# Sixteen f chunks of batches 0 and 1 as pairs of seven block products over token halves

## The chip, the cores and the metric

The kernel runs on one core of one Trainium2 chip. The metric is the device time of one execution in microseconds, lower is better. The engines are named as in the profile: PE (matrix products), DVE (vector), ACT (activations), POOL, SP (here a DMA queue).

## What is computed

Sigmoid attention over 8 batches, 12 heads, 448 tokens, head size 64, followed by a gated feed-forward layer on 3584 tokens (d_model 768, d_ff 1536):

```python
scores = scale * q @ k.T - log(S);  attn = 1 / (1 + exp(-scores))
x = (attn @ v) with the heads side by side          # 3584 x 768
out = (maximum(x @ w_gate, 0) * (x @ w_val)) @ w_out
```

## The kernel before

Everything is in fp16 with fp32 sums in PSUM, which is eight banks of 512 fp32 columns; `bank(name)` takes the next bank of a ring, and `later` moves banks to the ring's end. The schedule is written by hand: on each engine, instructions run in the order in which the code issues them, and tiles carry the waits between engines.

**Attention.** A unit is one key chunk of 64 tokens of a group of four heads: `qk_unit` writes the scores of 448 queries into two banks (L238), and two sigmoids on ACT (L186) bring them to SBUF as PT. A batch has 21 units, three groups of seven. `pv` (L256) multiplies a group's seven PT with v, and `put_xT` on DVE (L183) writes the transposed result xT: 6 chunks of 128 model columns by 448 tokens.

**Rounds.** Batch b's units are cut into six bursts (for b = 1 of 3, 3, 3, 4, 4, 4 units; later of 4, 3, 4, 3, 4, 3), some with a pv of the group before in them. After each burst, PE does feed-forward work of earlier batches, until the next burst; `jobs` are other steps (loads, rel copies and DMA transposes of the next batch, sums) that go along with that work. The queue `gv_queue` holds the direct feed-forward chunks, `ffn_mix(n)` does n of them, `next_work` does the next entry of `work`, and `prepare` makes the sums for the entry after.

**Direct chunks.** For one of the 12 f chunks (128 columns of d_ff), `gv_product` (L321) makes the gate and the value, each six matmuls into a bank of its own; ACT takes the Relu (L333) and DVE multiplies (L342) into hT. Batch 0's tokens are taken in parts of 256 and 192, batch 1's in one of 448.

**Seven products.** Batches 2 to 7 are taken two at a time: gate and value weights, and the two halves of d_model, make a 2 x 2 block matrix, and two batches the other side. `gv_pair` does two f chunks with seven block products (Strassen's scheme in Winograd's form, L408) in place of eight. Its sums of weights come from `gate_sums` (in place in wv) and `unit_sums` on DVE (L399, L571), those of tokens from `batch_sums`. Three PSUM banks per chunk, u (called b in the code), g2 (c) and g1 (a), are copied or added into SBUF tiles gsb (L616, L620) between products; the first copy is on DVE (on ACT at the end of the kernel), the next two on ACT.

**Down.** `down_pair` does the same for the last product, two tiles of 128 tokens at a time, with four sums of w_out (`weight_sums`, tile T) and `token_sums` on DVE. Work entries are ("w", g, f) for `gv_pair`, ("y", g, p) for `down_pair`, and ("t", g, 6) for tile 6, which is left over and goes through `down` (L369) directly. g counts pairs of batches.

**Around the change.** Batches 0 and 1 are all direct: 20 queue entries of batch 0 in b = 1's rounds (4, 3, 3, 3, 3, 4), nine chunks of batch 1 in b = 2's (2, 2, 1, 1, 1, 2), three in b = 3's (1, 1, 1, then tile 6, then y1). `down_pair` y0 follows the last two chunks of b = 2. The token sums for y0 are made in b = 2's third round, weight sum 0 in its fifth, 1 and 2 in its sixth, 3 beside y0. `dma_transposes` are two copies to a tile rel on DVE (L221) and a DMA transpose on SP. `hold` makes POOL wait for such a transpose before it issues the next loads.

Of the kernel before, what the change touches and what calls it, by code (L numbers as in the profile page):

```python
# [10 lines left out]
FP32 = mybir.dt.float32  # L11
# [6 lines left out]
def kernel(  # L18
# [332 lines left out]
    def store(g, t, ysb, m0, m1, engines):  # L351
        if (g, t) in ((0, 0), (0, 1)):
            put_off.append((g, t, ysb, m0, m1, engines))
        else:
            stored(g, t, ysb, m0, m1, engines)
# [8 lines left out]
    def down(g, t):  # L364
        ysb = ysbp.tile([P, DM], FP32, tag="ysb", name="ysb")
        for nm, m0, m1 in (("ya", 0, 512), ("yb", 512, DM)):
# [12 lines left out]
        store(g, t, ysb, 0, DM, (nc.sync, nc.sync))  # L379

    HF, HM, HD = NFC // 2, DM // 2, NDC // 2
    late = {}
# [170 lines left out]


    def gate_sums(f0, f1):
        fs = slice(f0 * P, f1 * P)
        sub(wv[:, 0:HD, fs], wg[:, 0:HD, fs], wv[:, 0:HD, fs])

    def unit_sums(g, f):
        S1, S2, S4 = sums_tile(2 * P)
# [6 lines left out]
        sums[("w", g, f)] = S1, S2, S4  # L573

    def batch_blocks(g, ks):
        x1, x2 = xT_tiles[2 * g], xT_tiles[2 * g + 1]
# [13 lines left out]
    def gv_pair(g, f, beside, first_copy):  # L590
# [67 lines left out]
        else:  # L658
# [2 lines left out]
            gated_first()  # L661
            gated_second(0, 2 * NPP * P - S)

    gv_queue = deque()

    def push_gv(b, q0, qn, fs, act_relu=True):
# [4 lines left out]
        c0, c1 = HALVES[half]  # L671
        push_gv(0, 64 * c0, 64 * (c1 - c0), fs, act_relu)

    def ffn_mix(count, hooks=()):
        hooks = list(hooks)
        for left in range(count, -1, -1):
            while hooks and hooks[0][0] >= left:
                hooks.pop(0)[1]()
            if left:
                gv_queue.popleft()()  # L680


    nc.scalar.activation(gate[:], zeros[:, 0:2], AF.Sigmoid, bias=sig_bias, scale=qk_scale)
# [63 lines left out]
                after[(i, u)]()  # L747
    slots[5].pv()
    push_first(1, range(0, 4))
    for f0 in range(4, 12, 2):  # L750
        for half in range(2):
            push_first(half, range(f0, f0 + 2))


    order = [(g, c) for g in range(NG) for c in range(NCH)]

    def pv_finish(b):
        pv_group(b, NG - 1)
        if b < 2:
            push_gv(b, 0, S, range(NFC))  # L760

    first_psum.close()
    open_banks("ring1")
# [4 lines left out]
    def both(b, g):  # L768
        pe_transposes(b, g, 0)
        pe_transposes(b, g, 1)  # L770
# [5 lines left out]
        load_o()  # L776


    work = deque()

    pending = []

    def push_group(g):
        tail = [("y", g, p) for p in range(3)]
        if g != 2:
            tail.insert(0, ("y", g, NPP) if g == 3 else ("t", g, 2 * NPP))
        if g == 0:
            tail.insert(0, tail.pop(1))
        work.extend([("w", g, f) for f in range(0, NFC, 2) if g > 0] + tail)

    def prepare():
        if work:
            kind, g, i = work[0]
            if kind == "w":
                unit_sums(g, i)
            elif kind == "y":
                token_sums(g, i, 0, HF - 2 if FRESH.get(g) == i else HF)

    def next_work(jobs=(), alone=False, first_act=False, amid=None):
        kind, g, i = work.popleft()  # L800

        due = pending[:]
        del pending[:]

        def beside():
            for job in due + list(jobs):
                job()

        if kind == "y":
            down_pair(g, i, beside, prepare, not work, scaled_act if alone or first_act else scaled, amid)  # L810
        elif amid:
            raise ValueError(kind)
        elif kind == "w":
            gv_pair(g, i, lambda: (prepare(), beside()), nc.scalar.copy if alone else nc.vector.tensor_copy)
        else:
            beside()
            prepare()
            down(g, i)

    for b in range(1, B):  # L820
        if b == 1:
            cuts, pv_at = (0, 3, 6, 9, 13, 17, 21), {3: (0, 2), 5: (1, 2)}
        else:
            cuts, pv_at = (0, 4, 7, 11, 14, 18, 21), {0: (-1, 2), 2: (0, 2), 4: (1, 2)}
        bursts = list(range(len(cuts) - 1))
        inner = {}
        if b > 2:
            inner = {0: 1} if b % 2 == 0 else {2: 3, 3: 5} if b == B - 1 else {4: 5}
            for n in inner.values():
                bursts.remove(n)  # L830
        count = len(bursts)
        hooks = {}
        if b == 1:
            mix = (4, 3, 3, 3, 3, 4)
            hooks = {
                1: [(3, lambda: both(1, 1))],
                3: [(3, lambda: both(1, 2))],
                4: [(3, lambda: dma_transposes(2, 0)), (1, lambda: dma_transposes(2, 1))],
                5: [(4, late_loads)],
            }  # L840
        elif b == 2:
            mix = (2, 2, 1, 1, 1, 2)
            hooks = {
                2: [(0, prepare)],
                4: [(0, lambda: weight_sums(0))],
                5: [(1, lambda: weight_sums(1)), (0, lambda: weight_sums(2))],
            }
            open_late()
        elif b == 3:
            mix = (1, 1, 1, 0, 0)  # L850
        else:
            mix = (0,) * count

        def burst(n):
            for i, (g, c) in enumerate(order[cuts[n] : cuts[n + 1]]):
                if n in pv_at and i == pv_at[n][1]:
                    if n == 0:
                        pv_finish(b - 1)
                        if b == 2:
                            push_group(0)  # L860
                        elif b % 2 == 0:
                            push_group(b // 2 - 1)
                    else:
                        pv_group(b, pv_at[n][0])
                qk_unit(b, g, c)

        if b == 3:
            dma_transposes(3, 2)
            for args in put_off:
                stored(*args)  # L870
        for m in range(count):
            jobs = []
            burst(bursts[m])
            if m == 0 and b > 3:
                jobs.append(lambda: dma_transposes(b, 2))
            if b == 2 and m == count - 1:
                jobs.append(lambda: (dma_transposes(3, 0), dma_transposes(3, 1)))
            elif b == 3 and m == count - 1:
                jobs.append(lambda: dma_transposes(4, 1))
            elif 0 <= m - count + 2 and 3 < b < B - 1:  # L880
                jobs.append(lambda: dma_transposes(b + 1, m - count + 2))
            if b == 1:
                if m == 0:
                    load(2, 0, 1, "kq")
                    load(2, 1, 2, "kq")
                    load(2, 2, 3, "kq")
            elif m == 0 and b + 1 < B:
                if b == 3:
                    jobs.append(lambda: hold(3, 2))
# [8 lines left out]
            if b == 2 and m == count - 1:  # L898
                ffn_mix(mix[m], hooks[m])
                next_work(jobs + [lambda: weight_sums(3)], first_act=True)  # L900
            elif mix[m]:
                for job in jobs:
                    job()
                ffn_mix(mix[m], hooks.get(m, ()))
            else:
                next_work(jobs, amid=(lambda: burst(inner[m])) if m in inner else None)
            if b == 3 and m == count - 2:
                dma_transposes(4, 0)
            if b == 3 and m in (1, 3):
                for f in range(*((0, 8, 2), (8, NFC, 2))[m // 2]):  # L910
                    gate_sums(f, f + 2)
    pv_finish(B - 1)
    push_group(B // 2 - 1)
    next_work([lambda: batch_sums(B // 2 - 1, (1, HD))])
# [32 lines left out]
```

## Time and profile before

| | |
|---|---|
| median of 3 runs | 391.92 us (391.62 to 392.65) |
| span of the profiled execution, first to last instruction | 390.9 us |
| the profiled execution's own time beside it | not shown; the runs lie 0.7 to 1.7 us above the span |
| PE, DVE, ACT, POOL busy | 384.7, 283.4, 228.4, 50.1 us |
| granted PE clock | 0.998 |

The parts of the span by stage, with PE's busy time from the windows view: first batch's attention 0 to 29.7 us (27.5), b = 1's rounds 29.7 to 62.3 (32.6, no idle), b = 2's 62.3 to 98.9 (36.6, no idle), b = 3's 98.9 to 135.7 with y1 in it (36.8, no idle), later rounds to 303.5 (167.8 of 167.8), and the end without attention (83.4 of 87.4). In profile lines an engine's idle time and what ended it stand in brackets, "x6" is the number of instructions in a row, and L321 is line 321 of the kernel.

### The profile page before, as it was taken

To read this page: it belongs to the slowest core of one execution; us is meant where nothing else is said; L and a number is where in the kernel's file an instruction comes from. 1 tells how busy PE (TensorE), PEld (TensorE's weight loads), DVE (VectorE), ACT (ScalarE), POOL (GpSimd) and SP (SyncE) were. 2 spreads that over 40 slices of the span, in tenths; PEclk is the share of its full clock that TensorE was granted. 3 is DMA by queue.
4 is the path that set the end of the run, shared out by engine and by line. 5 is a ranking of instruction groups with operands and counts; after the bars stand their busy time and mean duration, and the time that the engine had idled before them with its cause. 6 is when DMAs were issued, how large, how long until landed. Compare 5 with 4: busy or idle time off the path is not lost.

```text
span 390.9 us, 8798 instructions
## 1 busy us (share of the span) xinstructions
PE 384.7 (98%) x3504; PEld 218.0 (56%) x3504; DVE 283.4 (73%) x560; ACT 228.4 (58%) x483; POOL 50.1 (13%) x74
## 2 busy tenths in 40 slices
PE   8999999999999999999999999999999999999995
PEld 6678776445455545454555554545455555555663
DVE  3453444358387789999757789999987788999563
ACT  5967786784877755555556774545467354333321
POOL 8643404300320300003000300000000000000000
PEclk9999999999999999999999999999999999999999
DMA  9999997996998992225946696132003220000335
GB/s 174 198 199 204 204 186 120 205 204 111 194 185 166 140 236 37 49 47 58 195 93 115 136 198 108 24 67 41 14 18 74 74 80 2 0 3 0 81 88 155
DMA packets 68985, 43.79 MB, mean 112 GB/s; under 512 B 35664, under 2 KB 65616, under 8 KB 68944
## 3 DMA queue, kind: packets, MB, share of 16 engines
q0 software_dynamic: 30496, 23.24, 39.6%
q1 hardware_dynamic: 37664, 19.24, 24.1%
q10 hardware_dynamic: 784, 0.75, 0.6%
q8 instruction: 27, 0.44, 0.5%
q14 instruction: 14, 0.11, 0.1%
HBM read 47.19 MB, written 11.01 MB: 149 GB/s over the span
## 4 chain that ended last, share of the span: by engine, by line
PE 93%; DMA 4%; DVE 1%; POOL 1%; issue 0%; ACT 0%; POOLq 0%; DVEq 0%; ACTq 0%
PE u L408 33%; PE g L408 16%; PE y L408 10%; PE qk_ps L238 9%; PE pv_ps L256 7%; PE g_ps L321 7%; PE v_ps L321 7%; DMA wv<-in_moe_w_val_dram 3%; DMA k<-in_k_dram 2%; PE ya L369 1%; PE trt L203 1%; PE yb L369 1%; ACT PT L186 0%; DVE ysb L478 0%; POOL wg L148 0%
## 5 line engine op out<-in xcount | busy, mean ns | idle before, releaser
L186 ACT ACTIVATE PT<-qk_ps 128x448 f16<-128x448 f32 (+3 forms) x318 | 151.0, 585 | 75.2 <-PE qk_ps L238 75.0
L408 PEld LDWEIGHTS <-S 128*128 128x128 f16 x558 | 54.6, 98 | 44.7
L620 DVE TENSOR_TENSOR gsb<-g,gsb 128x448 f32<-128x448 f32 x72 | 42.9, 625 | 10.3 <-PE g L408 9.7
L238 PE MATMUL qk_ps<-qkT 64*64 64x448 f16 (+2 forms) x756 | 48.0, 337 | 0.5 <-ACT PT L186 0.3
L342 DVE TENSOR_TENSOR hT<-gate_sb,v_ps 128x256 f16<-128x256 f32 (+2 forms) x36 | 16.4, 465 | 35.5 <-PE v_ps L321 17.9
L408 PEld LDWEIGHTS <-hT 128*128 128x128 f16 x306 | 28.7, 98 | 22.3 <-issue 4.9
L616 ACT COPY gsb<-u 128x448 f32<-128x448 f32 x48 | 25.6, 557 | 24.0 <-PE u L408 22.9
L460 ACT ACTIVATE ysb<-u 128x384 f32<-128x384 f32 x31 | 15.2, 491 | 38.2 <-PE u L408 33.8
L256 PE MATMUL pv_ps<-PT,v 64*64 64x448 f16 (+2 forms) x756 | 37.2, 329 | 0.0
L183 DVE TENSOR_SCALAR xT<-pv_ps 128x448 f16<-128x448 f32 (+2 forms) x53 | 27.8, 567 | 10.9 <-PE pv_ps L256 9.8
L321 PE MATMUL v_ps<-xT,wv 128*128 128x256 f16 (+2 forms) x216 | 33.2, 290 | 0.5 <-DMA wv<-in_moe_w_val_dram 0.5
L321 PE MATMUL g_ps<-xT,wg 128*128 128x256 f16 (+2 forms) x216 | 33.3, 291 | 0.0
L408 PEld LDWEIGHTS <-wg 128*128 128x128 f16 x216 | 20.1, 98 | 21.8 <-issue 4.3
L408 PEld LDWEIGHTS <-wv 128*128 128x128 f16 x216 | 21.1, 98 | 19.7
L238 PEld LDWEIGHTS <-qkT 64*64 64x64 f16 x756 | 18.2, 106 | 21.2 <-issue 14.9
L478 DVE SCALAR_TENSOR_TENSOR ysb<-y,ysb 128x384 f32<-128x384 f32 x29 | 16.1, 556 | 17.9 <-PE y L408 10.4
L256 PEld LDWEIGHTS <-v 64*64 64x64 f16 x756 | 22.3, 107 | 10.6 <-issue 0.8
L408 PE MATMUL u<-T,hT 128*128 128x384 f16 x132 | 25.1, 326 | 0.0
L110 POOL DMA_DIRECT2D k<-in_k_dram x14 | 10.8, 773 | 111.0 <-DVE rel L221 104.2
L321 PEld LDWEIGHTS <-wg 128*128 128x128 f16 x216 | 18.8, 98 | 10.8 <-issue 4.5
L321 PEld LDWEIGHTS <-wv 128*128 128x128 f16 x216 | 20.1, 98 | 8.2 <-DMA wv<-in_moe_w_val_dram 0.8
L408 PE MATMUL u<-xT,wg 128*128 128x448 f16 x108 | 23.5, 354 | 0.0
(78 smaller groups left out, 536.4 us busy)
## 6 DMA issues: line engine op xcount, KB each, us to landing
out_dram<-ysb SPq DMA_DIRECT2D x52, 192.0 KB, 2.9
v<-in_v_dram POOLq DMA_DIRECT2D x8, 336.0 KB, 14.5
v<-in_v_dram POOLq DMA_DIRECT2D x16, 168.0 KB, 14.4
k<-in_k_dram POOLq DMA_DIRECT2D x4, 672.0 KB, 12.0
q<-in_q_dram POOLq DMA_DIRECT2D x4, 672.0 KB, 15.6
k<-in_k_dram POOLq DMA_DIRECT2D x9, 224.0 KB, 11.9
q<-in_q_dram POOLq DMA_DIRECT2D x7, 224.0 KB, 12.2
wo<-in_moe_w_out_dram POOLq DMA_DIRECT2D x1, 1536.0 KB, 12.0
```

The source lines that it names most:

```text
L110: nc.gpsimd.dma_start(t16[:, xs, cs], rows_of(src, b)[:, xs, cs])
L183: nc.vector.tensor_scalar(out=xT, in0=src, scalar1=XSCALE, scalar2=None, op0=AOP.mult)
L186: nc.scalar.activation(PT_ap, ps_ap, AF.Sigmoid, bias=sig_bias, scale=qk_scale)
L238: nc.tensor.matmul(out_of(hh)[o : o + 64, :], qkT[rows, c, cols], qkT[rows, NCH + c0 : NCH + c1, cols], start=True, stop=True, tile_positi ...
L256: nc.tensor.matmul(ps[hh][64 * r : 64 * r + 64, 0:qn], v16[rows, 2 * g + hh, c * D : (c + 1) * D], pieces[c][rows, hh, :], start=(c == 0), ...
L321: nc.tensor.matmul(ps[:, 0:qn], (wg, wv)[i][:, dc, f * P : (f + 1) * P], xT_tiles[b][:, dc, q0 : q0 + qn], start=(dc == 0), stop=(dc == ND ...
L342: nc.vector.tensor_tensor(out=hT_tiles[g][:, f, o : o + qn], in0=gate_sb[:, 0:qn], in1=ps[1][:, 0:qn], op=AOP.mult,)
L408: nc.tensor.matmul(ps[:, 0:n], A[:, k_, :], W[:, k_, :], start=(first and k_ == 0), stop=(k_ == kn - 1), skip_group_check=True,)
L460: nc.scalar.activation(o, ps[:, 0:HM], AF.Copy, scale=OUT_SCALE)
L478: nc.vector.scalar_tensor_tensor(out=o, in0=ps[:, 0:HM], scalar=OUT_SCALE, in1=o, op0=AOP.mult, op1=AOP.add)
L616: by(gs[u][i][:], ps[u][:, 0:S])
L620: nc.vector.tensor_tensor(out=gs[u][i][:], in0=ps[u][:, 0:S], in1=gs[u][i][:], op=AOP.add)
```

## The change

Batch 0's chunks 6 to 11 and batch 1's chunks 0 to 3 and 6 to 11 go through a new `gv_split`: two f chunks at a time, seven block products, the other side being the two token halves (224 tokens) of the same batch. Both chunks' results lie side by side in one bank. `split_sums` makes four sums of xT per batch on DVE. The sums of weights for f 6, 8 and 10 are made once, early, into tiles of the first stage, and serve both batches. Batch 0's chunks 0 to 5 and batch 1's 4 and 5 stay direct.

b = 1's rounds become a written plan (direct entries 4, 3, none, 1, none, none, and a split pair in the third, fifth and sixth). b = 2's rounds are chunk 4 of batch 1, splits 6, 8, 10, chunk 5, y0; b = 3's are splits 0 and 2, tile 6 in two parts of 320 and 448 columns, y1. The weight sums 0 and 1 move beside chunk 5, 2 and 3 beside y0; y0's token sums are made after chunk 5; y0's first copy stays on ACT. From b = 4 on nothing changes.

```diff
+    def gv_split(b, f, beside):
+        x = xT_tiles[b]
+        T1, T2, T4, T3 = split_X[b]
+        B11, B21, B22 = x[:, 0:HD, 0:SQ], x[:, HD:NDC, 0:SQ], x[:, HD:NDC, SQ:S]
+        p, c, a = (bank(nm) for nm in ("u", "g2", "g1"))
+        later((7, 6, 5))
+        gs = [gsbp.tile([P, S], FP32, tag="gsb", name="gsb") for _ in range(3)]
...
+        def product(ps, i, W, first=True):
+            for u in range(2):
+                for k_ in range(HD):
+                    nc.tensor.matmul(
+                        ps[:, u * SQ : (u + 1) * SQ], sets[u][i][:, k_, :], W[:, k_, :],
+                        start=(first and u == 0 and k_ == 0), stop=(k_ == HD - 1),
...
+        def copy(i, ps):
+            nc.scalar.copy(gs[i][:], ps[:, 0:S])
+        def plus(i, ps):
+            nc.vector.tensor_tensor(out=gs[i][:], in0=ps[:, 0:S], in1=gs[i][:], op=AOP.add)
...
+        product(p, 0, B11)
+        copy(0, p)
+        product(c, 3, T1)
+        copy(2, c)
+        product(p, 4, T2, False)
+        copy(1, p)
+        beside()
+        product(a, 1, B21)
+        plus(0, a)
+        product(p, 5, T3, False)
+        plus(2, p)
+        product(c, 6, B22, False)
+        plus(1, c)
+        product(p, 2, T4, False)
+        o = (b % 2) * S
+        gated(o, gs[0], p)
+        gated(o + SQ, gs[1], gs[2])
...
+    DOWN_CUTS = ((0, 320), (320, DM))
+    SPLIT, ULAST = (6, 8, 10, 0, 2), (4, 5)
...
+        if g == 0:
+            work.extend([("u", 1, ULAST[0]), *(("s", 1, f) for f in SPLIT[0:3]), ("u", 1, ULAST[1]), tail[0]])
+            work.extend([*(("s", 1, f) for f in SPLIT[3:5]), ("t", g, 0), ("t", g, 1), *tail[1:]])
+            return
...
+        elif kind == "s":
+            gv_split(g, i, lambda: (prepare(), beside()))
+        elif kind == "u":
+            gv(g, 0, S, i, True)
+            prepare()
+            beside()
...
+            plan = (
+                [4, lambda: split_sums(0)],
+                [lambda: both(1, 1), 3, lambda: early_unit_sums(0, 6)],
+                [lambda: gv_split(0, 6, idle)],
+                [lambda: both(1, 2), 1, lambda: early_unit_sums(1, 8)],
+                [
+                    lambda: dma_transposes(2, 0),
+                    lambda: gv_split(0, 8, lambda: early_unit_sums(2, 10)),
+                    lambda: dma_transposes(2, 1),
+                ],
+                [late_loads, lambda: gv_split(0, 10, idle)],
+            )
...
+                jobs += [
+                    lambda: dma_transposes(3, 0), lambda: weight_sums(2),
+                    lambda: dma_transposes(3, 1), lambda: weight_sums(3),
+                ]
...
+            if b == 2 and m == 0:
+                jobs.append(lambda: split_sums(1))
+            elif b == 2 and m == 4:
+                open_late()
+                jobs.append(lambda: (weight_sums(0), weight_sums(1)))
+            elif b == 3 and m == 2:
+                jobs.append(lambda: gate_sums(4, 6))
```

More of the change, by code (lines that the diff above doesn't have):

```diff
@@ L362, in stored, with down @@
             eng.dma_start(dst, ysb[64 * i : 64 * i + 64, m0:m1])
-    def down(g, t):
-        ysb = ysbp.tile([P, DM], FP32, tag="ysb", name="ysb")
-        for nm, m0, m1 in (("ya", 0, 512), ("yb", 512, DM)):
+    down_tiles = {}
+    def down(g, t, m0, m1):
+        if m0 == 0:
+            down_tiles[(g, t)] = ysbp.tile([P, DM], FP32, tag="ysb", name="ysb")
+        ysb = down_tiles[(g, t)]
+        for nm in ("yb" if m0 else "ya",):
             ps = bank(nm)
@@ L378, in down @@
             )
-        store(g, t, ysb, 0, DM, (nc.sync, nc.sync))
+        if m1 == DM:
+            store(g, t, ysb, 0, DM, (nc.sync, nc.sync))
     HF, HM, HD = NFC // 2, DM // 2, NDC // 2
@@ L561, in gate_sums, with early_unit_sums, unit_sums @@
     def gate_sums(f0, f1):
+        gates_done.update(range(f0, f1))
         fs = slice(f0 * P, f1 * P)
         sub(wv[:, 0:HD, fs], wg[:, 0:HD, fs], wv[:, 0:HD, fs])
-    def unit_sums(g, f):
-        S1, S2, S4 = sums_tile(2 * P)
+    def early_unit_sums(j, f):
+        views = []
+        for i in range(3 * j, 3 * j + 3):
+            t = early.tile([P, 2, 512], FP16, tag=f"PT{i}", name="S")
+            flat = t[:].rearrange("p a y -> p (a y)")[:, 0 : HD * 2 * P]
+            views.append(flat.rearrange("p (x y) -> p x y", y=2 * P))
+        unit_sums(("s", f), f, views)
+    gates_done = set()
+    def unit_sums(key, f, tiles=None):
+        if f not in gates_done:
+            gate_sums(f, f + 2)
+        S1, S2, S4 = tiles or sums_tile(2 * P)
         fs = slice(f * P, (f + 2) * P)
@@ L572, in unit_sums @@
         sub(S4, A12, S2)
-        sums[("w", g, f)] = S1, S2, S4
+        sums[key] = S1, S2, S4
     def batch_blocks(g, ks):
@@ L662, in gv_pair, with split_sums @@
             gated_second(0, 2 * NPP * P - S)
+    SQ = S // 2
+    split_X = {}
+    def split_sums(b):
+        tile_ = xTp.tile([P, NPAIR, S], FP16, tag="xT", name="X2")
+        flat = tile_[:].rearrange("p a s -> p (a s)")
+        T1, T2, T4, T3 = (
+            flat[:, i * HD * SQ : (i + 1) * HD * SQ].rearrange("p (k s) -> p k s", s=SQ) for i in range(4)
+        )
+        split_X[b] = T1, T2, T4, T3
+        x = xT_tiles[b]
+        B11, B21, B12, B22 = x[:, 0:HD, 0:SQ], x[:, HD:NDC, 0:SQ], x[:, 0:HD, SQ:S], x[:, HD:NDC, SQ:S]
+        sub(T1, B12, B11)
+        sub(T2, B22, T1)
+        sub(T4, B21, T2)
+        sub(T3, B22, B12)
@@ new lines, in gv_split, with gated @@
+    def gv_split(b, f, beside):
+        x = xT_tiles[b]
+        T1, T2, T4, T3 = split_X[b]
[3 more added lines that the diff above has]
+        gs = [gsbp.tile([P, S], FP32, tag="gsb", name="gsb") for _ in range(3)]
+        h = hT_tiles[b // 2]
+        sets = []
+        for u in range(2):
+            us, fs = slice(u * P, (u + 1) * P), slice((f + u) * P, (f + u + 1) * P)
+            S1, S2, S4 = (t[:, :, us] for t in sums[("s", f)])
+            sets.append((
+                wg[:, 0:HD, fs], wg[:, HD:NDC, fs], wv[:, HD:NDC, fs],
+                S1, S2, wv[:, 0:HD, fs], S4,
+            ))
+        def product(ps, i, W, first=True):
+            for u in range(2):
+                for k_ in range(HD):
+                    nc.tensor.matmul(
+                        ps[:, u * SQ : (u + 1) * SQ],
+                        sets[u][i][:, k_, :],
+                        W[:, k_, :],
+                        start=(first and u == 0 and k_ == 0),
+                        stop=(k_ == HD - 1),
+                        skip_group_check=True,
+                    )
+        def copy(i, ps):
+            nc.scalar.copy(gs[i][:], ps[:, 0:S])
+        def plus(i, ps):
+            nc.vector.tensor_tensor(out=gs[i][:], in0=ps[:, 0:S], in1=gs[i][:], op=AOP.add)
+        def gated(o, gate_sb, val):
+            gate_sb, val = (t[:, 0:S].rearrange("p (u s) -> p u s", u=2) for t in (gate_sb, val))
+            nc.vector.scalar_tensor_tensor(
+                out=h[:, f : f + 2, o : o + SQ], in0=gate_sb, scalar=0.0, in1=val, op0=AOP.max, op1=AOP.mult
+            )
+        product(p, 0, B11)
[15 more added lines that the diff above has]
+        gated(o + SQ, gs[1], gs[2])
@@ L672, in push_first, with ffn_mix, idle @@
         push_gv(0, 64 * c0, 64 * (c1 - c0), fs, act_relu)
[L674 to L680, printed above, removed]
+    def ffn_mix(count):
+        for _ in range(count):
+            gv_queue.popleft()()
+    def idle():
+        pass
     nc.scalar.activation(gate[:], zeros[:, 0:2], AF.Sigmoid, bias=sig_bias, scale=qk_scale)
@@ L749 @@
     push_first(1, range(0, 4))
-    for f0 in range(4, 12, 2):
-        for half in range(2):
-            push_first(half, range(f0, f0 + 2))
+    push_first(0, range(4, 6))
+    push_first(1, range(4, 6))
     order = [(g, c) for g in range(NG) for c in range(NCH)]
@@ L758, in pv_finish @@
         pv_group(b, NG - 1)
-        if b < 2:
-            push_gv(b, 0, S, range(NFC))
     first_psum.close()
@@ L784, in push_group @@
         tail = [("y", g, p) for p in range(3)]
+        if g == 0:
+            work.extend([("u", 1, ULAST[0]), *(("s", 1, f) for f in SPLIT[0:3]), ("u", 1, ULAST[1]), tail[0]])
+            work.extend([*(("s", 1, f) for f in SPLIT[3:5]), ("t", g, 0), ("t", g, 1), *tail[1:]])
+            return
         if g != 2:
[L786 to L789, printed above, removed]
+            tail.insert(0, ("y", g, NPP) if g == 3 else ("t", g, 2))
+        work.extend([("w", g, f) for f in range(0, NFC, 2)] + tail)
     def prepare():
@@ L794, in prepare @@
             if kind == "w":
-                unit_sums(g, i)
+                unit_sums(("w", g, i), i)
+            elif kind == "s" and ("s", i) not in sums:
+                unit_sums(("s", i), i)
             elif kind == "y":
@@ L817, in next_work @@
             prepare()
-            down(g, i)
+            for m0, m1 in (DOWN_CUTS[i : i + 1] if g == 0 else ((0, 512), (512, DM))):
+                down(g, 2 * NPP, m0, m1)
     for b in range(1, B):
@@ L831 @@
         count = len(bursts)
-        hooks = {}
         if b == 1:
[L834 to L852, printed above, removed]
+            plan = (
[9 more added lines that the diff above has]
+                [late_loads, lambda: gv_split(0, 10, idle)],
+            )
         def burst(n):
@@ L876 @@
             if b == 2 and m == count - 1:
-                jobs.append(lambda: (dma_transposes(3, 0), dma_transposes(3, 1)))
+                jobs += [
+                    lambda: dma_transposes(3, 0), lambda: weight_sums(2),
+                    lambda: dma_transposes(3, 1), lambda: weight_sums(3),
+                ]
             elif b == 3 and m == count - 1:
@@ L897 @@
                 jobs.append(lambda: batch_sums(b // 2 - 1, (1, HD)))
[L898 to L904, printed above, removed]
-            else:
-                next_work(jobs, amid=(lambda: burst(inner[m])) if m in inner else None)
+            if b == 1:
+                for step in plan[m]:
+                    if callable(step):
+                        step()
+                    else:
+                        ffn_mix(step)
+            else:
+                next_work(
+                    jobs,
+                    first_act=b == 2,
+                    amid=(lambda: burst(inner[m])) if m in inner else None,
+                )
             if b == 3 and m == count - 2:
                 dma_transposes(4, 0)
-            if b == 3 and m in (1, 3):
-                for f in range(*((0, 8, 2), (8, NFC, 2))[m // 2]):
-                    gate_sums(f, f + 2)
     pv_finish(B - 1)
```

## The prediction

> **What bounds the kernel now.** I read the page first: the busy times by engine and the chain that ended last.
>
> ```profile
> span 390.9 us, 8798 instructions
> PE 384.7 (98%) x3504; PEld 218.0 (56%) x3504; DVE 283.4 (73%) x560; ACT 228.4 (58%) x483; POOL 50.1 (13%) x74
> PE 93%; DMA 4%; DVE 1%; POOL 1%; issue 0%; ACT 0%; POOLq 0%; DVEq 0%; ACTq 0%
> ```
>
> PE is busy 98% of the span and is 93% of the chain; its waits in the list of waits come to 2 us. So a column taken off PE shortens the kernel, and a wait put on PE lengthens it by its whole size: there is no idle time for it to fall into. The change does both, so the next view is the timeline, for what a product costs.
>
> ```profile
> 60.22 0.66 PE L321 MATMUL g_ps<-xT,wg 128*128 128x192 f16 x6
> 60.71 0.66 PE L321 MATMUL v_ps<-xT,wv 128*128 128x192 f16 x6
> ...
> 69.84 1.31 PE L321 MATMUL g_ps<-xT,wg 128*128 128x448 f16 x6
> 70.98 1.30 PE L321 MATMUL v_ps<-xT,wv 128*128 128x448 f16 x6
> ```
>
> The columns are start, length, engine, line. Start to start, six matmuls of 192 columns take 0.495 us (82.5 ns each, 60.71 to 61.21 too), six of 448 take 1.137 (189.5), six of 256 take 0.655 (109.2): columns divided by 2.4 per ns, and 2.5 ns. A result is complete some 0.16 us after the next product has begun (1.30 against 1.14).
>
> Third, the same timeline around three kinds of bursts (scores on PE, sigmoids on ACT) and the first f chunk after each:
>
> ```profile
> 50.69 1.03 PE L238 MATMUL qk_ps<-qkT 64*64 64x448 f16 x16
> 51.12 3.60 ACT L186 ACTIVATE PT<-qk_ps 128x448 f16<-128x448 f32 x8 [0.59 <-PE qk_ps L238]
> 51.72 0.81 PE L321 MATMUL g_ps<-xT,wg 128*128 128x256 f16 x6
> 54.53 0.91 ACT L333 ACTIVATE gate_sb<-g_ps 128x256 f32<-128x256 f32 x3
> ...
> 64.50 1.31 PE L321 MATMUL g_ps<-xT,wg 128*128 128x448 f16 x6
> 66.13 0.62 ACT L333 ACTIVATE gate_sb<-g_ps 128x448 f32<-128x448 f32 x1
> ...
> 69.57 2.73 ACT L186 ACTIVATE PT<-qk_ps 128x448 f16<-128x448 f32 x6 [0.91 <-PE qk_ps L238]
> 72.13 0.60 ACT L333 ACTIVATE gate_sb<-g_ps 128x448 f32<-128x448 f32 x1
> ```
>
> A burst leaves ACT a queue of six or eight sigmoids, and whatever is written behind them on ACT starts late: counted from the chunk's first matmul, 2.81 us after a burst of four units, 1.63 where a pv lies in the burst (64.50 to 66.13), 2.29 after a burst of three (69.84 to 72.13). Now no PE instruction waits for that late Relu soon, since a direct chunk takes fresh banks.
>
> Fourth, the groups by shape, for the vector steps:
>
> ```profile
> L616 ACT COPY gsb<-u 128x448 f32<-128x448 f32 x48 | 25.6, 557 | 24.0 <-PE u L408 22.9
> L620 DVE TENSOR_TENSOR gsb<-u,gsb 128x448 f32<-128x448 f32 x36 | 21.5, 625 | 0.2
> ```
>
> **PE work removed.** A direct pair of chunks is 24 x 189.5 ns = 4.55 us in batch 1 and 24 x (109.2 + 82.5) ns = 4.60 in batch 0. A split pair is 42 matmuls of 224 columns. No weight-changing row has that size; 192 and 256 bound it at 82.5 and 109.2, the line through them gives 95.9, and the four warm-up matmuls of 224 columns at 10.21 (0.56 us) fit it. I take 95.9: 0.575 us per product, 4.03 per pair. Five pairs of batch 1 and three of batch 0 go from 36.5 to 32.2: 4.3 us saved.
>
> **The waits that the split adds.** gv_split has one bank each for p, c and a, and both chunks lie side by side in it. Product 3 adds into p, so it must wait until ACT has copied the whole of p; product 5 waits for the second copy of p, product 7 for plus(2, p) on DVE. PE takes its matmuls in order, so all later products and the next burst queue behind each wait. In gv_pair the same steps have two banks and products twice as long (1.14 us), and its first copy is on DVE; here a product lasts 0.575 and a copy still 0.557. The walk behind a burst of three, from the first matmul, with 0.04 us to hand over:
> - products 1 and 2 issue until 1.15. ACT reaches copy(0, p) at 2.29 and is done at 2.89.
> - product 3 at 2.94 (**wait 1.79**) to 3.52, complete 3.68; copy(1, p) 3.72 to 4.28; meanwhile product 4 until 4.09.
> - product 5 at 4.33 (**wait 0.24**) to 4.91, complete 5.07; plus(2, p) 5.11 to 5.73; product 6 until 5.48.
> - product 7 at 5.78 (**wait 0.30**) to 6.36.
>
> So 6.36 us: 4.03 and 2.33 of waits. From product 3 on it only shifts with ACT's queue: 6.88 after four units without a pv, 5.70 with one. The eight pairs: f 6 of batch 0 and f 6, 10 and 2 of batch 1 stand behind a burst of three, 4 x 6.36; f 8 of batch 0 behind four units, 6.88; f 10 of batch 0 and f 8 and 0 of batch 1 behind four and a pv, 3 x 5.70. Sum 49.4 against 36.5 direct: **+12.9 us**. The unknown is bounded: the column price moves only the three products between waits (0.24 per pair, 2 us in all), the hand-over could be 0.1 (six per pair, up to 3 us).
>
> **down_pair y0 loses its lead.** Now the first weight sums are long ready when y0 begins:
>
> ```profile
> 87.43 1.35 DVE L399 TENSOR_TENSOR T<-wo 128x2304 f16<-128x2304 f16 x1
> 90.93 1.35 DVE L399 TENSOR_TENSOR T<-wo,T 128x2304 f16<-128x2304 f16 x1
> ...
> 91.95 1.14 PE L408 MATMUL u<-wo,hT 128*128 128x384 f16 x6
> 92.93 1.14 PE L408 MATMUL y<-T,S 128*128 128x384 f16 x6
> ```
>
> T's first sum at 87.43 is 5 us ahead of its reader at 92.93, since two direct chunks stand in between. After the change, f 5 of batch 1, one burst of three and then y0 follow each other, and on DVE the order is: f 5's product (it waits for its v_ps), the four token sums (2.2 us at 79.78), weight sums 0 and 1. From f 5's first matmul: v_ps complete 2.43, product until 3.1, token sums until 5.3, sum 0 until 6.65, sum 1 until 7.95. PE: chunk 2.28, burst 0.70, y0 at 3.06, its second product wants sum 0 at 4.04 and gets it at 6.70 (**2.65**), the third 0.32 more. Behind these DVE has four rel copies and sums 2 and 3 (until 12.05) before its two plus steps, so the product on T3 waits 0.1 and the last one, for the second plus at 13.2, waits **1.25**. Sum **+4.3 us**, bounded by 0 (DVE runs ahead) and 5.
>
> **At nothing.** Tile 6 in 320 and 448 columns is the same 12 x 768; its cover is PE's 3.84 and 2.97 us in these rounds against 3.4 and 2.6 of sigmoids. DVE gains eight subtractions of 672 columns (between 0.39 at 448 and 0.55 at 768 columns) and five sets of three at 0.55, 12 us, and early gate sums; they run while DVE waits for PE, and where c needs S1 of f 6 and f 8 of batch 0 (1 us late) ACT's queue is later still. Without that cover it is that 1 us each. The rel copies and SP transposes of batch 2 move with the splits, and on POOL hold(2, 2), which gates v of batch 2 and wo: it comes some 4.5 us later, but so does the first pv that reads v, 11.6 us behind it now (63.31 to 74.88) for 4.7 us from issue to landing.
>
> Total 12.9 + 4.3 = +17.2: the profiled span of 390.9 becomes 408.1. The page gives no time beside the span; the median of the runs, 391.92, is 1.0 above it, so **409.1 us**.
>
> **Rivals.**
> 1. *y0 is covered*, DVE getting to the weight sums earlier: 391.9 + 12.9 = 404.8. For it: DVE is busy only 73%. Against: its order is fixed. 0.13.
> 2. *ACT's queue is no bound*, because copies find ACT free: then product 3 waits only for the copy itself (0.24), a pair is 4.81 and eight are 38.5, +1.9; with y0's 4.3, 398. Against: all eight pairs stand straight behind a burst. 0.12.
> 3. *PE's clock drops in the waits.* The trace begins at half pace: 22 matmuls of 194 columns in 3.74 us, 160 ns each for 83; later the granted clock is 1.00 throughout, but no gap here is long enough to test it. If the longest waits (2.3 and 2.65) each brought such a stretch back, +1.9 us each: 413. 0.07. The Trainium skill, TensorE: Matmul & The Clock Gate, section Part 1: The HAM clock gate, has the clock halve after an idle window of about 3.4 us; by that rule none of these waits is long enough and the time stays at 409.1; the half pace at the start agrees with it, and no gap in this trace shows its length.
> 4. *Faster*: the waits are hidden and only the columns count, 391.9 - 4.3 = 387.6. It decides at a wait of 0.54 us per pair: above that the split loses. Against it, even a free ACT leaves 0.78 (0.24 + 0.24 + 0.30). 0.04.
> 5. The waits just eat the saving, or the new products do not replace the old (PE would not go to x3576): no change, 0.02.
>
> My forecast has 0.62. 0.3% (1.2 us) is about what a measurement of this kernel can tell from no change. The range goes from 400, which is rival 1 with the two unknowns of 2 and 3 us on the cheap side, to 414, above rival 3 and above the forecast with the same unknowns on the dear side; outside are rivals 2, 4 and 5 (0.18). Faster 0.04, same 0.02, slower 0.94.
>
> **What would show it.** Right: PE busy falls from 98% to about 93%; the list of waits has PE waiting for ACT gsb (some 14 to 16 us over 16 waits, the longest 2.3), for DVE gsb (2.4 over 8) and for DVE T (near 3); PE has x3576; split products start 0.575 us apart; after y0 the rounds are as long as before. Wrong: PE near 98% (then rival 4 or 2), no wait on T (rival 1), a granted clock under 0.98 (rival 3).

## The result, and the profile after

The changed kernel takes **409.66 us** (median of 4 runs, 408.97 to 410.43) against 391.9 (391.62 to 392.65) of the kernel before: a ratio of 1.0453 [1.0436, 1.0471], slower. The forecast was 409.1. The execution behind the page after has a span of 407.5 us and took 409.28; the one behind the page before has 390.9 and took 392.65. So the spans grew by 16.6 us, where the sum had 17.2. Three executions far off the others, one of the changed kernel with direct pairs (663.59 us at a granted clock of 0.559, the only one of that kernel with a profile, which is not read) and two of the kernel before (404.01 and 1394.66 us), are left out of the medians here and below.

The page of the changed kernel, its busy times and its chain:

```profile
span 407.5 us, 8988 instructions
PE 385.5 (95%) x3576; PEld 225.2 (55%) x3576; DVE 307.3 (75%) x601; ACT 231.1 (57%) x485; POOL 50.1 (12%) x74
PE 85%; ACT 9%; DVE 3%; issue 2%; DVEq 0%; ACTq 0%
```

There are 72 matmuls more. PE's busy time did not fall by the 4.3 us of columns, it rose by 0.8: a product counts as busy until its result is complete, 0.16 us after the next could have begun, so each of the new waits (three a pair) hides up to 0.16 us, some 4 us in all, and 1.5 us of half pace come on top (below). In the chain PE's share went from 93% to 85% and ACT's from 0% to 9%. The list of PE's waits names the places (waited for, us in total, times, longest):

```profile
PE u L713 <- ACT gsb L723: 10.2, 8, 1.7
PE y L407 <- DVE T L398: 2.4, 1, 2.4
PE u L713 <- DVE gsb L726: 2.0, 8, 0.6
PE g L713 <- DVE S L583: 1.3, 2, 0.8
```

Before, no such line existed. One split pair in the timeline, f 6 of batch 1, behind a burst of three as in the prediction's walk (start, length, engine, line; the brackets hold the idle time before it and what ended it):

```profile
71.44 2.73 ACT L186 ACTIVATE PT<-qk_ps 128x448 f16<-128x448 f32 x6 [0.61 <-PE qk_ps L238]
71.65 0.75 PE L713 MATMUL u<-xT,wg 128*128 128x224 f16 x6
...
74.00 0.59 ACT L723 COPY gsb<-u 128x448 f32<-128x448 f32 x1
...
74.65 0.73 PE L713 MATMUL u<-X,S 128*128 128x224 f16 x6 [1.67 <-ACT gsb L723]
...
78.19 0.38 PE L238 MATMUL qk_ps<-qkT 64*64 64x448 f16 x4
```

The copy is behind six sigmoids and begins 2.35 us after the first product (the walk had 2.29); product 3 begins at 3.00 (walk 2.94) and the next burst at 6.54, of which 0.09 is the step to the scores (walk 6.36 without it). The list counts idle time only from the end of the last result, so its eight waits of 1.7 and less are some 0.16 us longer from issue to issue each, and product 5's wait is not in it at all: it begins 0.78 after product 4 (75.22 to 76.00) where 0.575 is the pace.

y0, the other place:

```profile
100.88 1.35 DVE L398 TENSOR_TENSOR T<-wo 128x2304 f16<-128x2304 f16 x1
...
102.28 2.08 PE L407 MATMUL y<-T,S 128*128 128x384 f16 x6 [2.40 <-DVE T L398]
104.16 1.74 PE L407 MATMUL u<-T,S 128*128 128x384 f16 x6
105.73 1.14 PE L407 MATMUL y<-wo,hT 128*128 128x384 f16 x6
```

The sum T is made at 100.88, when PE already waits; before, it lay 5 us ahead. And after the wait six matmuls of 384 columns take 1.88 us (102.28 to 104.16), then 1.57, where 0.975 is their time. In the windows the granted clock (the column behind POOL) is half there:

```profile
102.30:105.20 2.90, 2.90 (x10) 1.35 (x10) 2.90 (x4) 0.49 (x1) 0.00 (x0) 0.50 0.00 0
```

By sections the added 16.6 us are: eight split pairs 51.1 us from their first product to the next burst, against 37.3 for the same pairs before (three of 4.70, five of 4.64): **+13.8**. y0 10.99 against 6.95: **+4.0**. All else -1.2, of which 0.9 lie at the start, where only loads differ. From y1 on nothing changed.

### The profile page after: what moved, and what is told of

The parts are those of the page before. It is cut to its first block, busy times and chain, and to the rows that moved or that the text cites. A ratio compares the mean times of both kernels' runs of the same rounds, so it can differ in the third digit from the quotient of the medians.

```text
span 407.5 us, 8988 instructions
## 1 busy us (share of the span) xinstructions
PE 385.5 (95%) x3576; PEld 225.2 (55%) x3576; DVE 307.3 (75%) x601; ACT 231.1 (57%) x485; POOL 50.1 (12%) x74
## 4 chain that ended last, share of the span: by engine, by line
PE 85%; ACT 9%; DVE 3%; issue 2%; DVEq 0%; ACTq 0%
PE u L407 32%; PE g L407 15%; PE y L407 10%; PE qk_ps L238 8%; ACT PT L186 7%; PE pv_ps L256 7%; PE u L713 4%; PE g_ps L321 2%; PE v_ps L321 2%; ACT gsb L723 2%; DVE gsb L726 1%; PE warm_ps L174 1%; PE trt L203 1%; PE ya L373 1%; PE yb L373 1%
## 5 line engine op out<-in xcount | busy, mean ns | idle before, releaser
L632 DVE TENSOR_TENSOR gsb<-g,gsb 128x448 f32<-128x448 f32 x72 | 42.8, 624 | 10.1 <-PE g L407 9.5
L407 PEld LDWEIGHTS <-wg 128*128 128x128 f16 x216 | 20.1, 98 | 21.8 <-issue 4.3
L407 PEld LDWEIGHTS <-wv 128*128 128x128 f16 x216 | 21.1, 98 | 19.7
L726 DVE TENSOR_TENSOR gsb<-g,gsb 128x448 f32<-128x448 f32 x16 | 9.9, 619 | 18.4 <-PE g L713 18.4
L407 PE MATMUL g<-xT,S 128*128 128x448 f16 x108 | 23.4, 352 | 0.0
L407 PE MATMUL u<-X,S 128*128 128x448 f16 x108 | 23.4, 352 | 0.0
L407 PE MATMUL u<-xT,wv 128*128 128x448 f16 x108 | 23.4, 353 | 0.0
L407 PE MATMUL u<-X,wv 128*128 128x448 f16 x108 | 23.4, 352 | 0.0
## 6 DMA issues: line engine op xcount, KB each, us to landing
q<-in_q_dram POOLq DMA_DIRECT2D x7, 224.0 KB, 12.2
wo<-in_moe_w_out_dram POOLq DMA_DIRECT2D x1, 1536.0 KB, 12.9
```

Of the source, the lines that this page charges most:

```text
L407: nc.tensor.matmul(ps[:, 0:n], A[:, k_, :], W[:, k_, :], start=(first and k_ == 0), stop=(k_ == kn - 1), skip_group_check=True,)
L632: nc.vector.tensor_tensor(out=gs[u][i][:], in0=ps[u][:, 0:S], in1=gs[u][i][:], op=AOP.add)
L726: nc.vector.tensor_tensor(out=gs[i][:], in0=ps[:, 0:S], in1=gs[i][:], op=AOP.add)
```

## The experiments

Two theories stood at the start. The one of the prediction: the waits of the split pairs and y0's lost lead make the whole loss, and each can be undone by itself. Its rival: the new order of the rounds (rounds without direct chunks, the moved copies and transposes) costs a good part.

**Direct pairs in the changed schedule.** The split pairs are computed as direct chunks, everything else stays where the change put it; the sums that only the splits need are left out.

```diff
+    def direct_pair(b, f):
+        parts = [(64 * c0, 64 * (c1 - c0)) for c0, c1 in HALVES] if b == 0 else [(0, S)]
+        for q0, qn in parts:
+            for u in range(2):
+                gv(b, q0, qn, f + u, True)
-                [lambda: gv_split(0, 6, idle)],
+                [lambda: direct_pair(0, 6)],
```

> The changed kernel's schedule, with every split pair done as two direct chunks. Theory (the split's waits cost 13.8 us: its eight pairs take 51.1 us from first product to next burst in the trace after, direct ones 37.3): about 395.9 us, with y0's wait on T still there (2.4 us and the half clock behind it). Rival (the rest of the schedule costs it, not the split): above 402 us.

Measured: **396.06 us**, ratio 1.0105 [1.0077, 1.0133]. The split costs 409.66 - 396.06 = 13.6 us, by subtraction; 13.8 by the trace. The rest, 4.3 over the kernel before, stays with the direct pairs, so it belongs to the order and not to the split. The rival's time, above 402, is not reached: the order costs a quarter of the loss, and y0 is most of that (below).

**The first copy on DVE.** As `gv_pair` has it: the first copy no longer stands behind ACT's sigmoids.

```diff
-        copy(0, p)
+        copy(0, p, nc.vector.tensor_copy)
```

> The changed kernel with only copy(0, p) on DVE in place of ACT. Theory (ACT's sigmoids hold the first copy): where DVE is free (f 6, 10, 2 and 8 of batch 1) product 3's wait falls from 1.7 or 1.0 us to under 0.4, product 5 then waits some 0.8 for the second copy, still behind the sigmoids; about 0.9 us less for each of these, nothing where DVE has sums in front (batch 0, f 0): 406.1 us. Rival (42 short matmuls are dear in themselves): 409.7, no change.

Measured: **405.27 us**, ratio 1.0334 [1.0311, 1.0357], 4.4 us under the changed kernel. Its waits of PE:

```profile
PE u L713 <- DVE gsb L723: 3.7, 5, 1.3
PE u L713 <- ACT gsb L723: 1.3, 2, 0.7
```

ACT's 10.2 us became 5.0: the copy now waits in DVE's queue where the sums of the token halves are ahead of it (1.3 at f 6 of batch 1, where under 0.4 was expected), and at two pairs the second copy, still on ACT, is late in its place. ACT's queue is a cause, but a copy that moves to the other engine meets that engine's queue.

**y0's lead given back.** Weight sum 0 ahead of the burst before y0, two of the rel copies and sum 1 behind it, the other copies at y0's end.

```diff
+            if b == 2 and m == 4:
+                open_late()
+                weight_sums(0)
             burst(bursts[m])
+            if b == 2 and m == 4:
+                dma_transposes(3, 0)
+                weight_sums(1)
```

> The changed kernel with weight sum 0 ahead of the fifth round's burst, the first rel copies and sum 1 behind it ahead of chunk 5, and the second rel copies at y0's end. Theory (DVE's order delays T): y0 falls from 11.0 us to about 8.1, the clock stays at 1.00, 406.7 us. If the clock drop had nothing to do with the wait, it stays and 1.5 us of this are missing. Rival (opening the late tiles delays T, not DVE's order): 409.7.

Measured: **406.45 us**, ratio 1.0367 [1.0343, 1.0391], 3.2 under the changed kernel. y0's first two products:

```profile
99.15 1.15 PE L407 MATMUL u<-wo,hT 128*128 128x384 f16 x6
100.40 1.15 PE L407 MATMUL y<-T,S 128*128 128x384 f16 x6
```

The wait on T is gone, and so is the half pace: y0 takes 7.92 us instead of 10.99, and the granted clock of the run is 1.000. Some 1 us over the kernel before stays at y0: 0.27 at its second product, and at its third a wait of 0.6 in the list for ACT's ysb.

**Units of scores between the products.** With y0's lead, the products in the order 1, 4, 3, 2, 5, 6, 7 and the burst's own units put between them, to fill the waits with work that PE has to do anyway; the second copy on DVE.

```diff
+        product(p, 0, B11)
+        copy(0, p)
+        product(a, 1, B21)
+        plus(0, a)
+        between(units[0:1])
+        product(p, 4, T2, False)
+        nc.vector.tensor_copy(gs[1][:], p[:, 0:S])
+        held.pop(1)
+        c = take("g2")
+        product(c, 3, T1)
+        copy(2, c)
+        between(units[1:2])
```

> e3, and in each split the burst's units and its pv stand between the products (product 1, product 4, a unit, 3, 2, a unit, 5, a unit or pv, 6, rest, 7) with the second copy on DVE, so that the first copy is ahead of the sigmoids on ACT. Theory (the loss is waits, not products): waits of 0.1 to 0.4 us per pair, and some 1 to 2 us in all where weight sums come late on DVE; 393.5 us, between 390 and 397. Rival (the products themselves are dear): above 404.

Measured: **406.79 us**, ratio 1.0388 [1.0338, 1.0437]. This expectation failed, by 13 us, and the time is where the rival had it (above 404), though the trace gives other reasons than dear products. There are three. One round has no wait listed, f 10 of batch 1, and it is still no gain:

```profile
84.75 0.74 PE L727 MATMUL g<-xT,wg 128*128 128x224 f16 x6
85.42 0.38 PE L238 MATMUL qk_ps<-qkT 64*64 64x448 f16 x4
```

From a product to a unit of scores 0.67 us pass, 0.095 over the product's 0.575, and a unit by itself takes 0.31 to 0.42, where three in a burst take 0.70 together. With its three units and four such steps the round takes 5.47 us (84.17 to 89.64); a burst of three and a direct pair took 5.34 before (69.14 to 74.48). Seven products save 0.52 and the taking apart of the burst costs 0.65. The Trainium skill, TensorEngine Tiling (Array Packing), section Key Properties, says that a change of tiling mode (the scores use 64 x 64 tiles, the products the whole array) drains the engine; the 0.095 agrees with it. Second, PE waited for DVE's gsb 4.9 us over 6 and for its sums S 1.7 over 2, which queue behind each other there. Third, y0 waited 2.5 for S on DVE, and PE 1.5 for a transpose of rel: a copy rel had waited 2.75 on DVE for a load of q, with the token sums behind it. So this run does not test the walk of the split; it shows that waits filled in this way have a price of their own, and that my count of it was nothing.

**Both orders right, without the split.** Direct pairs with y0's lead.

> e1 and e3 together: the changed schedule with direct pairs and y0's sums ahead. Theory (two separate losses that add): 396.4 - 3.2 = 393.1 us, PE busy 98% again, and what is left over 391.9 is y0's remaining 0.9 us of waits. Rival (the two hide each other, or a third loss sits in the rearranged rounds): 395 or more.

Measured: **394.66 us**, ratio 1.0082 [1.0066, 1.0098]. Taken as separate, the two parts would leave 392.9 (13.6 + 3.2 off 409.66), so 1.8 us do not add, and the time is nearer to the rival's 395 than to the theory's 393.1. Of the 2.9 over the kernel before, 2.0 lie at y0 (8.99 us against 6.95), which waits 1.7 for S: as with the units between, a copy rel waited 1.9 on DVE for a load of q, with the token sums behind it. So this third loss comes from the loads' place in the order, which the prediction had at nothing.

**Own banks.** Each chunk of a split pair has banks of its own, as in `gv_pair`, so that a product can begin when its own chunk's copy, half as long, is done.

```diff
-        p, c, a = (bank(nm) for nm in ("u", "g2", "g1"))
+        p, c, a = ([bank(nm) for _ in range(2)] for nm in ("u", "g2", "g1"))
```

> The changed kernel with a PSUM bank of its own for each of a pair's two chunks, as in gv_pair: each copy, addition and gate step is then two of 224 columns. Theory (in one shared bank a copy can't begin before both chunks' products are through): product 5's wait of 0.21 us and product 7's of 0.37 nearly go, product 3's falls by 0.2; ACT's sigmoids stay in front of the first copy. Some 0.6 us per pair, 405 us. Rival (only ACT's queue counts, and more instructions on ACT and DVE cost as much as is won): 409 to 411.

Measured: **404.36 us**, ratio 1.0313 [1.03, 1.0327], 5.3 under the changed kernel. In the trace the pairs took 46.3 us instead of 51.1, though one of them, f 8 of batch 0, lost 1.6 to a half pace that the changed kernel had at y0 instead (last section). The same pair as above:

```profile
73.75 0.73 PE L407 MATMUL u<-X,S 128*128 128x224 f16 x6 [1.48 <-ACT gsb L719]
74.32 0.74 PE L407 MATMUL g<-xT,wg 128*128 128x224 f16 x6
```

From here on products are 0.575 apart (74.32, 74.90, 75.47, 76.05): products 5 and 7 wait no more, so these waits were the shared bank's. Product 3 still waits 1.48 for ACT, whose queue is as it was. In this run y0 kept full pace behind the same 2.40 us of idle time, and its later waits can be read:

```profile
99.29 1.14 PE L407 MATMUL y<-T,S 128*128 128x384 f16 x6 [2.40 <-DVE T L398]
...
105.36 1.14 PE L407 MATMUL u<-T,hT 128*128 128x384 f16 x6 [0.60 <-DVE ysb L477]
```

**All three cures together.** Own banks, first copy on DVE, y0's lead.

> The changed kernel with everything found so far against its waits: each chunk of a split pair has banks of its own, the first copy of a pair runs on DVE, and y0's weight sums, the copies rel and the transposes of the next batch lie where they give y0 its lead back. Nothing of the work is left out. Theory (the columns are saved as predicted, 0.5 us a pair, and the loss is made of three waits that can be taken away one by one: the copy behind the sigmoids, the shared bank, y0's sums): eight pairs at 4.03 to 4.3 us and y0 at 7 to 8 us. From the direct kernel with the lead (394.66) eight pairs would take 4.2 us off and DVE would give back 1 to 3 us where a first copy meets the token halves' sums (1.29 us at one pair where DVE had the copy): 392.5 us, range 390.5 to 396; PE's wait for gsb in the list of waits falls from 12 us to under 4. Rival (the waits are not removed but handed on, as in the kernel with units between the products, since DVE's queue takes ACT's place): PE waits for DVE gsb instead, 6 us or more, and the time stays above 398.

Measured: **398.87 us**, ratio 1.0181 [1.0167, 1.0196]: above the range of the theory and just above the rival's 398, though DVE's waits for gsb are not the rival's 6 us. PE's waits in the list:

```profile
PE u L407 <- DVE gsb L719: 2.1, 3, 1.1
PE u L407 <- DVE gsb L723: 1.6, 2, 0.8
PE u L407 <- ACT gsb L719: 1.6, 2, 0.8
```

With S (1.1), xT (0.7) and ysb (0.6) that is 7.7 us. The cures work in part: 12.2 us of waits for gsb became 5.3, and y0 takes 8.19 us. But the eight pairs take 43.2 us start to start, 37.3 as direct chunks: +5.9, and y0 +1.2, together the whole 7.1 over the kernel before (391.78). Many short waits in both queues took the place of three causes: a product of 0.575 us leaves its copy or sum little time to come second in a queue. In this form the split loses even then.

**Products twice as long.** The kernel before, with only batch 1's chunks 4 to 7 split, as two pairs side by side: each of the seven steps is done for both pairs, so that 1.15 us pass between a product and the step that needs its copy. The weight sums for it are made early, as in the change; everything else is direct.

```diff
+        def product(ps, i, W, first=True):
+            for j in range(2):
+                for u in range(2):
+                    for k_ in range(HD):
+                        nc.tensor.matmul(
+                            ps[j][:, u * SQ : (u + 1) * SQ],
...
-            mix = (2, 2, 1, 1, 1, 2)
+            mix = (1, 4, 1, 1, 1, 1)
+            elif b == 2 and m == 1:
+                gv_double(1, 4, rest[0])
```

> The kernel before, with four of batch 1's chunks (4 to 7) as two split pairs side by side in one round, product for product in turn (1.15 us between a bank's products), first copies on DVE; that round has four chunks and two others one less. Theory (the scheme pays where the other pair's products cover the copies): 4 x 2.27 = 9.1 us of direct products become 8.06 and no wait is left; 390.9 us, 0.25% under the kernel before. Rival (waits or DVE's sums eat it even so): 391.9 or more.

Measured: **391.32 us** (12 runs) against 391.72 (17 runs), ratio 0.9992 [0.9983, 1.0]: between the theory's 390.9 and the rival's 391.9, and hardly to be told from no change. In the round itself nothing waits:

```profile
67.85 1.32 PE L711 MATMUL u<-xT,wg 128*128 128x224 f16 x12
69.01 1.31 PE L711 MATMUL g<-S 128*128 128x224 f16 x12
```

Seven such steps and the way to the scores take 8.15 us (67.85 to 76.00), four direct chunks 9.10 and 0.09: the 1.0 us of columns is there. Part of it went again into y0 (7.37 against 6.95), where the third weight sum lay behind a direct chunk's last step on DVE, with the rel copies behind it.

**The same, weight sums one round earlier.**

```diff
-                3: [(0, lambda: weight_sums(0))],
-                4: [(0, lambda: weight_sums(1))],
-                5: [(0, lambda: weight_sums(2))],
+                2: [(0, lambda: (open_late(), prepare(), weight_sums(0)))],
+                3: [(0, lambda: weight_sums(1))],
+                4: [(0, lambda: weight_sums(2))],
```

> The kernel before with batch 1's chunks 4 to 7 as two split pairs side by side (391.32 us against 391.72 of the kernel before), and the three weight sums ahead of y0 moved one round earlier each, so that on DVE the copies rel for batch 3 are not behind the third sum. Nothing of the work is left out. Theory (the double pair saves 1.0 us and 0.4 to 0.6 of it went into y0 and the round behind it, since a sum came late there): y0 back to 7.0 us, no wait on the transposes of rel behind it, 390.7 us (390.0 to 391.3), 0.3% under the kernel before. Rival (what was given back does not hang on the order of the sums, but lies in the loads at the start and in later rounds): 391.3 as before.

Measured: **390.98 us** (11 runs) against 391.78 (14 runs), ratio **0.9978 [0.9969, 0.9987]**: the one version that is faster than the kernel before, by 0.2%, and clear of the noise. y0 and the round behind it:

```profile
91.29 1.14 PE L408 MATMUL y<-T,S 128*128 128x384 f16 x6
...
97.23 0.57 PE L238 MATMUL qk_ps<-qkT 64*64 64x448 f16 x8
```

y0 takes 6.92 us (from 90.32) and neither it nor the next burst waits. Under the kernel before of their own comparison the two versions stand 0.40 and 0.80 us; the difference, 0.40, is about that of the y0s (0.45).

## Why the prediction was right, by its steps

- **What bounds the kernel.** Right: PE was the bound, and waits put on it came out in the span at full size.
- **PE work removed.** The price of a 224-column product, which no comparable row of before had, was right: 0.575 us (74.32, 74.90, 75.47, 76.05 with own banks; 0.57 from 74.65 to 75.22 in the pair above, and 0.59 for the first product behind the scores). That seven products replace eight is seen alone in the double pair.
- **The waits of the split, +12.9.** The mechanism was right: ACT's queue at product 3, the shared bank at 5 and 7. Taking the one away saved 4.4 us, the other 5.3. The size was +13.8 by the trace and 13.6 by the run with direct pairs. The steps to the scores cancel between both sides (0.09 each). Of the 0.9 that is missing, half is one pair, f 0 of batch 1, whose last product waited 0.57 for plus(2, p) on DVE where the pair above has 0.21; the other seven were 0.02 to 0.11 longer each than the walk, as the hand-over from a copy's end to its reader was 0.05 to 0.06 us, not 0.04.
- **y0's lead, +4.3.** The sum came out (4.0), its parts only in part. The first wait was 2.57 issue to issue (2.65 predicted). Then the walk has 0.32, 0.1 and 1.25; what came was half pace for 2.9 us, worth 1.5, and under it the later sums had time to be ready. In the run with own banks, where the clock held, the later waits did come, 0.42 and 0.77 issue to issue, and y0 took 10.68: +3.7. So the four-wait walk was 0.6 too dear, by its last term (1.25 for 0.77; the 0.1 did not show), and the clock made up for half of that.
- **At nothing.** The early S sums were late at two places (1.3 us listed for S on DVE), where the walk had 1 us each under ACT's later queue; those pairs were 0.12 and 0.14 over it, 0.09 of it the step to the scores, so the cover held. Tile 6 and the loads cost nothing that shows in the changed kernel; with y0's lead given back the loads did show, at y0 (direct pairs with the lead, above).
- **The rivals.** Rival 3, the clock, came true in one of its two places: after the wait at y0, not after the eight of 1.7 us, at 1.5 us for the 1.9 that I gave it. It did not reach its 413: one stretch of half pace and not two, and at y0 it took the place of the later waits instead of adding to them. Its sign, a granted clock under 0.98, could not have shown it: one such stretch leaves 0.994. Rivals 1 and 2 had the copies or the sums in time; none was. For rival 4 I had said that even a free ACT leaves 0.78 per pair; with all cures together the new waits still took 1.3 us per pair start to start (43.2 us less eight times 4.03 and 0.09).
- **What would show it.** PE busy is 95%, not 93, since the ends of results count as busy. ACT gsb 10.2 us over 8, not 14 to 16 over 16: product 5's waits stay under the 0.16 us tail and are not listed. DVE gsb 2.0 over 8 for 2.4; DVE T 2.4 for 3. The gsb lines of the list come to 12.2 us; start to start the split's waits are 18 (13.8 and the 4.3 of columns).
- **The median.** I set 1.0 us between span and median; the profiled executions themselves took 1.75 and 1.78 us over their spans. The one before happened to be 0.7 above its median, the one after 0.4 below. So 16.6 between the spans are 17.8 between the medians, and the forecast's 17.2 lay between the two. That the total came within 0.6 us is in part luck: the pairs were 0.9 too cheap and y0 0.3 too dear, and the -1.2 elsewhere, 0.9 of it at the start, was in no term of the sum.

## What to carry to other kernels

A step that reads a bank back before the next product may add into it needs the product between them to be as long as the copy, its hand-over and the queue of the engine that does it. Halve the product and the waits return, whatever is saved in columns: here 0.52 us saved per pair met 2.3 us of waits, and the same algebra with steps of 1.15 us kept what it saved. Before giving a step to another engine to free it of a queue, read that engine's queue at that very place; and when direct work is replaced by shorter work, look at what the longer work had been giving time to (here y0's sums, 4 us).

## What the runs showed of the hardware

- **The clock falls after gaps much shorter than the longest harmless one.** At half pace for some 3 us: after 2.40 us of idle time at y0 (the changed kernel; also with the first copy on DVE, where it began a little later), and with own banks after waits of 0.34 and 1.32 in one pair:

```profile
53.72 1.28 PE L407 MATMUL u<-X,S 128*128 128x224 f16 x6 [1.32 <-ACT gsb L719]
54.80 1.32 PE L407 MATMUL g<-xT,wg 128*128 128x224 f16 x6
```

  Three products take 3.31 us there instead of 1.73. At full pace: after the same 2.40 at y0 with own banks, after 2.54 with units between, and after all eight waits up to 1.7 in the changed kernel. So the length alone does not decide. The Trainium skill, TensorE: Matmul & The Clock Gate, section Part 1: The HAM clock gate, asks for an idle window of about 3.4 us, and says that the window runs freely, so that the point of change depends on where in it the work falls. The traces here bear out the second and differ from the first. In all three kernels the half pace lasts 3.41 us and begins a whole number of 3.413 us stretches after the clock first rose: 28, 28 and 14 of them. I laid this grid over the ten profiles at full pace, up to the last matmul. Of 1143 stretches, seven held 0.85 to 1.24 us of matmuls (without the 0.16 us tails), and each was followed by half pace; four of these lie at the kernel's end. All others held 1.36 us or more, and none was. So the same 2.40 us at y0 counts in the changed kernel, where one stretch (98.54 to 101.96) holds nearly all of it and 1.09 us of matmuls, and not with own banks, where a border at 98.09 cuts it in two. This is an order found in the traces; no run moved the border on purpose. One of the four executions of the changed kernel had a granted clock of 1.000, so the half pace at y0 is not in every execution of the same kernel.
- **A step between full-array products and 64 x 64 units costs PE about 0.1 us**: 0.67 for 0.575 at each product that a unit follows, and a lone unit takes 0.31 and more, where a third of a burst of three is 0.23.
